# Tail queries of the last layer's attention: four accumulating matmuls per half of the keys, or one matmul per expert whose two halves are added afterwards

## The chip, the cores and the metric

The kernel runs on one core of a Trainium2 chip. The time is the device time of one execution in microseconds (us); the median of three runs of the kernel before is 1179.79 us (1178.86 to 1179.97). Engines are named as in the profile: PE is TensorE (PEld its weight loads), DVE is VectorE, ACT is ScalarE, POOL is GpSimd, SP is SyncE, which here only issues DMAs.

## The reference, cut to what matters

The program computes three layers one after the other: an attention over 32 memory slots, a token and channel mixer, and a mixture of four attention experts. The change lies in the third layer alone:

```python
for e in range(E):                                  # E = 4 experts, B = 8 batches, S = 576, Hd = 64
    q = x @ wq[e]; k = x @ wk[e]; v = x @ wv[e]
    scores = scale * (q @ k.transpose(0, 2, 1))     # 576 x 576 per batch and expert
    scores = np.where(causal, -1e9, scores)         # key j > query i is masked
    a = softmax(scores)
    ye = a @ v @ wo[e]
    out += gate(e) * ye                             # the two best experts of each token
```

Everything is float32. A value is held as a high and a low part (the float32r value that TensorE reads, and the remainder), and a product is built from products of the parts.

## The kernel before, in words

The last layer goes through 32 heads n = 4b + e (batch b, expert e), one per turn t of the loop at the end; a turn scores head t, and transposes and weighs head t-1. Between these steps, `some()` puts in pieces of work that do not belong to the head: the projections to q, k and v, the channel mixer of the next batch (`mm1_2`, `mm2_2`) and the output projection (`project`). The order in which each engine gets its instructions is not the order of the text: the program is built with `schedule_with_timeline_sim=True`, so that a scheduler lays out all engines on a timeline of planned durations and writes the order down; on the chip every engine then follows its written order and waits where an operand is late.

The 576 queries of a head are four blocks of 128 rows (`scores`, c = 0 to 3) and a tail of ST = 64. The tails of two experts, n and n+1 with n even, are handled together, expert n in partitions 0 to 63 and expert n+1 in 64 to 127. There are 16 such pairs.

For one head, `kk` holds the high part of the keys in one half of the partitions and the low part in the other. `qa` holds the queries so that `qa` times `kk` gives high times high plus low times low (the main terms), and `qb` so that `qb` times `kk` gives the two cross products. `tail_queries` (L1346) copies the 64 tail columns of `qa` and `qb` of both experts by four DMAs into `qz`, whose other columns were set to zero once at the start.

`tail_scores(n, hf)` is called for each half (hf) of the 576 keys, 288 columns each. It runs four matmuls into one PSUM tile `s` (L1357): two experts, main and cross terms. Because the other 64 columns of each operand are zero, all four add into one tile. `masked` (L1324) then reads the tile on DVE, adds the causal mask (`cmask`, zero for the first half, `tmask` for the second), scales, writes `ssb` and leaves the row's minimum in `nb`; the second half starts from the first half's minimum. After the second half ACT takes the exponential into `atl` (L1362).

`norm(n)` forms the factor `cf` on DVE (L1370 to L1372) from the sums of all blocks and of the tail and from the gates; POOL multiplies the four blocks of `a` by it (L1380), ACT the tail (L1376). Only then can PE transpose head n's blocks in `turn` (L1399, and L1401 for the last 64 tail columns), in the next turn; `tail_turn` (L1419) transposes the rest of the tail a turn later still.

For e = 2 the two calls of `tail_scores` stand between `scores`, `turn` and `weigh`. For e = 0 they stand between the value projections of a new batch, and the gates are computed after them. PSUM has eight banks here: three for `g`, two each for `t` and `s`, one for `y`.

The lines that the prediction speaks of:

```python
PE.matmul(p[:, 0:SH], lhsT=qz[:, i, x, :], rhs=kk[n + i][:, ks],            # L1357
          start=(i + x == 0), stop=(i + x == 2))
DVE.tensor_tensor_reduce(out=out, in0=p, in1=mask, scale=-scale, ...)       # L1324, masked
ACT.activation(atl[:, 0:S], s_[:], AF.Exp, scale=-1.0, bias=nb[:, 1:2], ...)# L1362
POOL.tensor_mul(x_, x_, cf[:, c:c + 1].to_broadcast([128, W]))              # L1380, norm
```

## Time and profile before

| | us |
|---|---|
| median of 3 runs | 1179.79 (1178.86 to 1179.97) |
| the profiled execution | 1177.93 |
| its span, first to last instruction | 1176.2 |
| PE busy in the span | 1155.9 |
| PEld, DVE, ACT, POOL busy | 1052.5, 785.0, 591.2, 407.8 |
| first and last tail matmul of the last layer (start) | 735.7, 1139.3 |

The profiled execution is 1.86 us below the median, and its span 1.7 us below its own time. Busy time of PE is the union of matmuls whose ends are modelled, so a busy PE can still have a lighter or denser stream of matmuls under it; how densely they follow one another is read from the starts of successive weight loads or matmuls. The granted clock of PE is 0.998 of full speed on the mean over the span.

### The profile page before, as it was taken

Reading aid. Unit: us, or ns where it says so; the run is one execution under the profiler, and the core shown is the slowest. Engines: PE = TensorE matmul, PEld = TensorE weight load, DVE = VectorE, ACT = ScalarE, POOL = GpSimd, SP = SyncE. Lnnn points to the kernel's source line nnn. Section 1 sums busy time; section 2 is a strip of 40 time slices with the busy share of each in tenths; the row PEclk is TensorE's granted clock in tenths of the full one; section 3 lists DMA queues with packets and bytes.
Section 4 is the critical chain, followed back from the end, with each engine's and each line's share of the span. In section 5 each row is a group of like instructions: output and inputs, shape, how many; then the busy total and the mean of one; then the engine's idle time right before and its main releaser. Section 6 shows DMA issues by size and latency. Waiting matters only on the chain.

```text
span 1176.2 us, 23497 instructions
## 1 busy us (share of the span) xinstructions
PE 1155.9 (98%) x8658; PEld 1052.5 (89%) x8658; DVE 785.0 (67%) x1942; ACT 591.2 (50%) x1533; POOL 407.8 (35%) x575
## 2 busy tenths in 40 slices
PE   7999999999999999999999999999999999999998
PEld 6788888888899999999998889999999999999986
DVE  6889998485565665746553624876666777687763
ACT  3566675442322231322221214777677767676774
POOL 3866766000101010100100544647272737373331
PEclk9999999999999999999999999999999999999999
DMA  8999974350121220303110453323332333222423
GB/s 255 248 268 288 285 238 167 133 172 36 38 70 36 72 79 30 108 1 108 37 64 35 131 151 106 90 67 97 77 100 73 103 95 110 70 84 72 151 88 108
DMA packets 125843, 133.53 MB, mean 114 GB/s; under 512 B 36000, under 2 KB 95392, under 8 KB 125728
## 3 DMA queue, kind: packets, MB, share of 16 engines
q1 hardware_dynamic: 125728, 132.03, 37.4%
q8 instruction: 68, 1.11, 0.4%
q14 instruction: 47, 0.39, 0.1%
HBM read 89.01 MB, written 31.46 MB: 102 GB/s over the span
## 4 chain that ended last, share of the span: by engine, by line
PE 83%; DVE 8%; DMA 2%; POOL 2%; issue 2%; ACT 2%; SPq 0%; ACTq 0%; DVEq 0%; POOLq 0%
PE g L251 24%; PE o L251 21%; PE h L251 19%; PE y L1444 4%; PE s L1335 3%; PE t L1399 3%; PE s L1357 1%; POOL a L1380 1%; PE g L677 1%; DVE cm L780 1%; DMA cst<-in_moe_w_tok_dram 1%; PE t L251 1%; PE g L680 1%; PE g L678 1%; PE g L671 1%
## 5 line engine op out<-in xcount | busy, mean ns | idle before, releaser
L983 POOL TENSOR_TENSOR tl<-ub,th 128x512 fp32r<-128x512 f32 x12 | 18.5, 1561 | 362.3 <-DVE tl L983 313.1
L251 PE MATMUL o<-hl,w2h 128*128 128x512 f32 x360 | 141.1, 392 | 0.0
L251 PE MATMUL o<-hh,w2l 128*128 128x512 f32 x360 | 140.4, 390 | 0.0
L251 PE MATMUL o<-hh,w2h 128*128 128x512 f32 x360 | 135.0, 392 | 0.0
L1380 POOL TENSOR_TENSOR a<-a,cf 128x128 f32<-128x128 f32 (+3 forms) x128 | 88.1, 721 | 69.0 <-DVE cf L1372 65.2
L935 ACT ACTIVATE hh<-m 128x256 fp32r<-128x256 f32 x120 | 48.9, 417 | 125.1 <-DVE m L1006 66.1
L1324 DVE CUSTOM_DVE_ANT_0 ssb<-s,cmask 128x128 f32<-128x128 f32 (+2 forms) x144 | 68.5, 483 | 25.2 <-PE s L1335 17.2
L1337 ACT ACTIVATE a<-ssb,nb 128x128 f32<-128x128 f32 (+3 forms) x128 | 71.4, 558 | 19.0 <-DVE nb L1324 14.9
L251 PEld LDWEIGHTS o<-hh,w2l 128*128 128x128 f32 x360 | 67.7, 188 | 14.5
L251 PEld LDWEIGHTS o<-hh,w2h 128*128 128x128 f32 x360 | 67.7, 189 | 12.3
L251 PEld LDWEIGHTS o<-hl,w2h 128*128 128x128 f32 x360 | 67.9, 189 | 11.9
L251 PE MATMUL h<-uh,w1l 128*128 128x256 f32 (+2 forms) x232 | 76.7, 332 | 0.0
L251 PE MATMUL h<-uh,w1h 128*128 128x256 f32 (+2 forms) x232 | 76.3, 331 | 0.0
L251 PE MATMUL h<-ul,w1h 128*128 128x256 f32 (+2 forms) x232 | 76.2, 332 | 0.0
L936 DVE SCALAR_TENSOR_TENSOR hl<-m,hh 128x256 fp32r<-128x256 f32 x120 | 58.7, 498 | 17.9 <-ACT hh L935 15.2
L251 PE MATMUL g<-xh,qkh 128*128 128x288 f32 x232 | 65.5, 301 | 0.0
L1236 POOL TENSOR_TENSOR xl<-p,xh 128x288 fp32r<-128x288 f32 x60 | 47.5, 810 | 49.5 <-ACT xh L1235 49.4
L251 PE MATMUL g<-xh,qkl 128*128 128x288 f32 x232 | 64.1, 296 | 0.0
L999 ACT ACTIVATE m<-h 128x256 f32<-128x256 f32 x30 | 11.5, 384 | 101.4 <-PE h L251 101.4
L1001 DVE TENSOR_TENSOR m<-m,h 128x256 f32<-128x256 f32 x30 | 12.6, 421 | 70.8 <-PE h L251 70.2
L258 DVE TENSOR_TENSOR Bl<-t,Bh 128x512 fp32r<-128x512 f32 (+1 forms) x80 | 50.5, 633 | 13.1 <-ACT Bh L255 12.1
L255 ACT ACTIVATE Bh<-t 128x512 fp32r<-128x512 f32 (+1 forms) x80 | 43.9, 552 | 14.8 <-PE t L1399 6.0
(332 smaller groups left out, 3816.5 us busy)
## 6 DMA issues: line engine op xcount, KB each, us to landing
cst<-in_moe_w_ch_dram SPq DMA_DIRECT2D x24, 512.0 KB, 4.0
u_d<-u SPq DMA_DIRECT2D x32, 288.0 KB, 3.1
ub<-u_d SPq DMA_DIRECT2D x9, 1024.0 KB, 5.0
u<-u_d SPq DMA_DIRECT2D x16, 576.0 KB, 4.1
p<-x_d SPq DMA_DIRECT2D x15, 576.0 KB, 4.0
qn<-in_q_dram SPq DMA_DIRECT2D x16, 512.0 KB, 5.5
kv<-in_k_dram SPq DMA_DIRECT2D x16, 512.0 KB, 5.8
kv<-in_v_dram SPq DMA_DIRECT2D x16, 512.0 KB, 5.6
```

The costliest lines, as they stand in the source:

```text
L251: PE.matmul(ps, lhsT=a, rhs=b, start=start and i == 0, stop=stop and i == len(seq) - 1)
L255: ACT.activation(hi, src, AF.Copy)
L258: DVE.tensor_sub(lo, src, f(hi))
L935: ACT.activation(hh, c, AF.Relu)
L936: DVE.scalar_tensor_tensor(hl, c, 0.0, f(hh), op0=OP.max, op1=OP.subtract)
L1236: POOL.tensor_sub(xl[b][:, c, ss], x_, f(xh[b][:, c, ss]))
L1324: DVE.tensor_tensor_reduce(out=out, in0=p, in1=mask, scale=-scale, scalar=least, op0=OP.add, op1=OP.min, accum_out=acc)
L1335: PE.matmul(p[:, 0:W], lhsT=q_[n][:, 128 * c:128 * c + 128], rhs=kk[n][:, 0:W], start=(i == 0), stop=(i == 1))
L1337: ACT.activation(a[:, aoff[c]:aoff[c] + W], s_[:, 0:W], AF.Exp, scale=-1.0, bias=nb[:, 0:1], accum_out=sm[:, c:c + 1])
L1380: POOL.tensor_mul(x_, x_, cf[:, c:c + 1].to_broadcast([128, W]))
L1399: PE.transpose(p[:, 128 * kc:128 * kc + 128], a[:, o + 128 * kc:o + 128 * kc + 128], ident[:])
L1444: PE.matmul(p[:, lo:w], lhsT=v_[:, kc, 0, :], rhs=x, start=(i == 0), stop=(i == len(ops) - 1))
```

## The change

Each expert's tail operand becomes one tile of 128 columns: main terms (from `qa`) in one half of the columns, cross terms (from `qb`) in the other. One matmul per expert gives both, main in the half of the partitions where that expert's tail belongs and cross in the other half. ACT copies the cross half out of PSUM into a new SBUF tile `cross`, in the partitions of the main half; `masked` then takes that tile where it took the mask. Keys 0 to 511 need no mask for the tail queries, so parts 0 and 1 (one expert each, 512 columns) have none; part 2 (keys 512 to 575 of both experts, 64 columns each in one PSUM tile) has POOL add a 64-column mask to the copied terms first. The zero fill of `qz` goes, and `tmask` shrinks to 64 columns. `tail_scores` is called three times instead of two: for e = 2 the third right after the second, for e = 0 after one more value projection.

```diff
-        tmask = wk_.tile([128, SH], F32, name="tmask")
-        POOL.tensor_copy(tmask[0:ST, :], cmask[0:ST, SH:S])
-        POOL.tensor_copy(tmask[ST:128, :], cmask[ST:128, SH + ST:S + ST])
-        qz = wk_.tile([128, 2, 2, 128], F32R, name="qz")
-        POOL.memset(f(qz[:]), 0.0)
+        tmask = wk_.tile([128, ST], F32, name="tmask")
+        POOL.tensor_copy(tmask[0:ST, :], cmask[0:ST, SM:S])
+        POOL.tensor_copy(tmask[ST:128, :], cmask[ST:128, S:S + ST])
+        qz = wk_.tile([128, 2, 128], F32R, name="qz")
...
-                    SP.dma_start(f(qz[:, i, x, ST * i:ST * i + ST]), f(q_[n + i][:, SM:S]))
+                    o = ST * (x ^ i)
+                    SP.dma_start(f(qz[:, i, o:o + ST]), f(q_[n + i][:, SM:S]))
-        def tail_scores(n, hf):
+        def tail_scores(n, part):
-            if hf == 0:
-                tails[n] = (wk_.tile([128, S], F32, name="ssb", bufs=2), wk_.tile([128, 2], F32, name="nb", bufs=4))
-            s_, nb = tails[n]
-            ks = slice(SH * hf, SH * hf + SH)
+            if part == 0:
+                tails[n] = (wk_.tile([128, S], F32, name="ssb", bufs=2), wk_.tile([128, 2], F32, name="nb", bufs=4),
+                            wk_.tile([128, S], F32, name="cross"))
+            s_, nb, x_ = tails[n]
             p = pp.tile([128, 512], F32, name="s", bufs=2)
-            for i in range(2):
-                for x in range(2):
-                    PE.matmul(p[:, 0:SH], lhsT=qz[:, i, x, :], rhs=kk[n + i][:, ks],
-                              start=(i + x == 0), stop=(i + x == 2))
-            masked(s_[:, ks], p[:, 0:SH], tmask[:] if hf else cmask[:, 0:SH], nb[:, hf:hf + 1],
-                   nb[:, 0:1] if hf else 3.0e38)
-            if hf:
+            ks = slice(0, SM) if part < 2 else slice(SM, S)
+            todo = []
+            for i in (part,) if part < 2 else range(2):
+                o = ST * i
+                c = p[:] if part < 2 else p[:, ST * i:ST * i + ST]
+                PE.matmul(c, lhsT=qz[:, i, :], rhs=kk[n + i][:, ks], start=True, stop=True)
+                ACT.activation(x_[o:o + ST, ks], c[ST - o:128 - o, :], AF.Copy)
+                todo.append((slice(o, o + ST), c))
+            if part == 2:
+                POOL.tensor_add(x_[:, ks], x_[:, ks], tmask[:])
+            for h, c in todo:
+                masked(s_[h, ks], c[h, :], x_[h, ks], nb[h, part // 2:part // 2 + 1], nb[h, 0:1] if part == 2 else 3.0e38)
+            if part == 2:
                 ACT.activation(atl[:, 0:S], s_[:], AF.Exp, scale=-1.0, bias=nb[:, 1:2],
                                accum_out=smb[n % 2][:, NQ - 1:NQ])
...
                 tail_scores(t, 1)
+                tail_scores(t, 2)          # e == 2
...
                 tail_scores(t, 1)
                 values(b, 3)
+                tail_scores(t, 2)          # e == 0
                 values(b, 4)
```

## Rows read from the trace of the kernel before

**Rows 1.** The page, part 1: busy us (share of the span) xinstructions of each engine.
```profile
PE 1155.9 (98%) x8658; PEld 1052.5 (89%) x8658; DVE 785.0 (67%) x1942; ACT 591.2 (50%) x1533; POOL 407.8 (35%) x575
```
**Rows 2.** Windows, last layer: length, busy of each engine, clock, DMA share, GB/s.
```profile
900.00:960.00 60.00, 60.00 (x449) 58.45 (x448) 42.69 (x134) 42.62 (x125) 29.85 (x46) 1.00 0.34 100
...
1150.00:1176.20 26.20, 20.35 (x112) 16.86 (x110) 8.66 (x19) 11.09 (x25) 4.14 (x7) 1.00 0.32 111
sum 486.20, PE 476.11 PEld 457.84 DVE 329.15 ACT 331.31 POOL 231.58; mean PE 47.61 PEld 45.78 DVE 32.91 ACT 33.13 POOL 23.16
```
**Rows 3.** PE's waits from 727 us on, longest of seven lines: total us, times, longest.
```profile
PE g L251 <- ACT osb L1497: 1.3, 3, 0.7
```
**Rows 4.** Timeline, weight loads of one pair's eight tail matmuls: start, us, instruction.
```profile
735.57 1.11 PEld L1357 LDWEIGHTS s<-kk,qz 128*128 128x128 f32 x8
736.62 0.19 PEld L251 LDWEIGHTS g<-hh,w2h 128*128 128x128 f32 x1
```
**Rows 5.** Timeline, a 64-column matmul, 512-column ones behind it, and their weight loads.
```profile
1140.40 0.22 PE L1444 MATMUL y<-Bt,vhl 128*128 128x64 f32 x1
1140.42 0.19 PEld L251 LDWEIGHTS g<-woh,yh 128*128 128x128 f32 x1
1140.45 0.48 PE L251 MATMUL g<-woh,yh 128*128 128x512 f32 x1
1140.53 0.19 PEld L251 LDWEIGHTS g<-wol,yh 128*128 128x128 f32 x1
...
1140.77 0.19 PEld L251 LDWEIGHTS g<-woh,yh 128*128 128x128 f32 x1
```
**Rows 6.** Groups by form, ACT and POOL: busy us, mean ns of one | idle before.
```profile
L1497 ACT ACTIVATE osb<-g 128x512 f32<-128x512 f32 x33 | 19.6, 597 | 13.3 <-DMA out_dram<-osb 5.9 <-PE g L251 5.4 <-ACT a L1337 0.5
...
L1281 ACT ACTIVATE vh<-g 64x64 fp32r<-64x64 f32 x8 | 1.6, 206 | 0.0
...
L1463 POOL TENSOR_TENSOR yel<-yt,yeh 128x64 fp32r<-128x64 f32 x16 | 5.3, 328 | 9.7 <-ACT yeh L1462 9.7
```
**Rows 7.** Groups by form, DVE, line of `masked`: the blocks' and the tail's.
```profile
L1324 DVE CUSTOM_DVE_ANT_0 ssb<-s,cmask 128x512 f32<-128x512 f32 x32 | 21.9, 685 | 0.8 <-PE s L1335 0.4
...
L1324 DVE DVE_READ_ACCUMULATOR2_ANT nb<- 128x1 f32 x160 | 13.2, 82 | 0.0
...
L1324 DVE CUSTOM_DVE_ANT_0 ssb<-s,cmask 128x128 f32<-128x128 f32 x32 | 9.3, 290 | 14.5 <-PE s L1335 14.0
L1324 DVE CUSTOM_DVE_ANT_0 ssb<-s,tmask,nb 128x288 f32<-128x288 f32 x16 | 8.2, 513 | 5.1 <-PE s L1357 4.8
L1324 DVE CUSTOM_DVE_ANT_0 ssb<-s,cmask 128x288 f32<-128x288 f32 x16 | 7.3, 454 | 3.9 <-PE s L1357 3.6
```
**Rows 8.** ACT's waits from 727 us on: total us, times, longest.
```profile
ACT kk L1256 <- DVE kk L1257: 6.5, 12, 1.6
```
**Rows 9.** Timeline of PE, second half of pair 8's tail scores.
```profile
838.41 0.56 PE L1357 MATMUL s<-kk,qz 128*128 128x288 f32 x3
...
839.93 0.38 PE L1357 MATMUL s<-kk,qz 128*128 128x288 f32 x1
```
**Rows 10.** Timeline of pair 8 (e = 0): the tail's sum on ACT, the factor on DVE.
```profile
841.60 0.19 ACT L1362 ACTIVATION_READ_ACCUMULATOR atl<-ssb,nb 128x1 f32 x1
...
850.56 0.16 DVE L1372 TENSOR_TENSOR cf<-cf,gate 128x5 f32<-128x5 f32 x1
```
**Rows 11.** Timeline of pair 30 (e = 2): factor, products, first transposes.
```profile
1142.38 0.17 DVE L1372 TENSOR_TENSOR cf<-cf,gate 128x5 f32<-128x5 f32 x1
...
1142.69 2.75 POOL L1380 TENSOR_TENSOR a<-a,cf 128x128 f32<-128x128 f32 x4 [6.84 <-DVE cf L1372]
...
1146.01 0.49 PE L1399 MATMUL t<-ident,a 128*128 128x128 f32 x3
```
**Rows 12.** Timeline, POOL at the layer's start: the pause after its fills.
```profile
703.03 0.81 POOL L1236 TENSOR_TENSOR xl<-p,xh 128x288 fp32r<-128x288 f32 x1 [11.26 <-ACT xh L1235]
```
**Rows 13.** Windows, 5 us from the first tail matmul of pair 2 (e = 2).
```profile
749.50:754.50 5.00, 5.00 (x40) 5.00 (x39) 4.29 (x12) 4.50 (x12) 5.00 (x8) 1.00 0.00 0
```

## The prediction

> **What bounds the kernel now.** I read the page's engine totals first: PE is busy 98% of the span, DVE 67%, ACT 50%, POOL 35% [rows 1]. Busy time alone is no proof, so next came the table of windows over the last layer, where the whole change lies. A window from its middle has PE busy 60.00 of 60 us, DVE and ACT about 42.6 each, POOL 29.9, with the clock at 1.00; only the last 26 us have PE at 20.35 [rows 2]. Then the waits: from 727 us to the end PE waits for another engine in seven groups, the longest of them 1.3 us in all [rows 3]. So in this layer time is what PE's written order takes to stream, matmul behind matmul, and the other engines have some 30% of room. A matmul taken away is time taken away, as long as what feeds PE is not made late.

> **What goes from PE.** Each of the 16 pairs has eight tail matmuls of 288 columns. Their duration (about 0.3 us) overlaps, so the price is the distance of their starts: the eight weight loads begin at 735.57 and the next instruction's at 736.62 [rows 4], 1.05 us a pair.

> **What comes to PE.** Two matmuls of 512 columns and two of 64. Loads of successive 512-column matmuls stand 0.24 us apart (1140.53 to 1140.77) [rows 5]: 0.48 a pair. For 64 columns there is a low and a high end. The only such matmul has its successor start 0.05 us after it (1140.40, 1140.45), but two loads in a row never stand closer than 0.11 there (1140.42, 1140.53) [rows 5], and two small ones in a row pay that. I take 0.08, between, since the second will often be apart from the first (below): 0.16 for two, 0.10 to 0.22. The sum is 0.64 (0.58 to 0.70) a pair, 0.41 saved (0.35 to 0.47), over 16 pairs **6.6 us (5.6 to 7.5)**.

> **What comes to the other engines.** ACT gets two copies of 64x512 and two of 64x64 out of PSUM. The nearest rows are 0.597 us for 512 columns and 0.206 for 64 [rows 6]: 1.61 us a pair, 26 in all. DVE loses 0.454 + 0.513 and two accumulator reads of 0.082; it gets two reductions over 512 columns at 0.685, two over 64, and four reads. The 64-column one is the 128-column row less 64 columns at the slope of the rows (0.395 us for 384 columns), 0.22 [rows 7]. That is 1.13 against 2.14, 1.0 more a pair, 16 in all. POOL gets one add of 128x64, 0.33 like the subtraction of that size [rows 6], 5 in all. The layer's sums go from 329 to 345 on DVE, 331 to 357 on ACT and 232 to 237 on POOL, of 486 us [rows 2]. None becomes the bound; I cost them at nothing because PE's stream covers them. With the cover gone they would cost at most what they are, 26 us by ACT.

> **Other edits.** The zero fill and the larger mask copies go from POOL at the layer's start; POOL then sits idle 11.26 us anyway [rows 12], so nothing either way. The four DMAs of a pair carry the same 64 columns each over the same queue. The new `cross` tile has one buffer, but pairs are over 10 us apart, so no pair waits for the last one's.

> **The added waits.** In part 2 ACT's first copy stands between the two small matmuls, and both work on one PSUM tile. Does the program keep the second matmul off while ACT reads other columns of it? ACT's copy of one expert's keys (L1256) waits 6.5 us for DVE's read of the other partitions of the same tile, from which it needs no value [rows 8], so yes: PE will wait there, with all later matmuls in its order behind it. The scheduler can put other work into that place, as it did in pair 8, where the second half's first three matmuls began at 838.41 and the fourth at 839.93 [rows 9]. If nothing is put there, the stop is a matmul of 0.22 [rows 5] and a copy of 0.206 [rows 6], 0.43 us a pair at least. I take 0.15 as given back per pair, near the covered end because rows 3 and 9 show covered waits, **2.4 us** in all (0 to 6.9 or more).
> [...]

> The second added wait is in the chain from the tail scores to the factor. Before, a reduction of 0.51 and its read of 0.08 followed the last matmul, 0.9 with that matmul's 0.3. After, it is matmul 0.22, copy 0.21, matmul 0.22, copy 0.21, add 0.33 and two reductions with reads, 0.60, together 1.8, and three more hand-overs at about 0.14 (1142.55 to 1142.69, factor to POOL [rows 11]): 1.3 us later. For e = 0 the tail's sum is ready at 841.8 and the factor is formed at 850.56, since the gates come last [rows 10]: 8.8 us hide it. For e = 2 the products end at 1145.44 and the transposes start at 1146.01 [rows 11], 0.57 us; whether PE then has something else decides the first rival.

> **Sum.** -6.6 + 2.4 = -4.2 us. From the profiled execution's 1177.93 that is 1173.7; this lies 1.86 below the median of the runs, so against the median **1175.6**.

> **Rivals.**
> 1. *The readers eat it.* For e = 2 the other engines are locally full: in 5 us from pair 2's first tail matmul DVE is busy 4.29, ACT 4.50, POOL 5.00 [rows 13], and 1.0, 1.6 and 0.33 come on top. If the transposes are late by 1.3 - 0.57 = 0.73 us for the eight pairs with e = 2 and PE has nothing to put there, 5.8 us come back: 1179.0. For it: the small reserve. Against it: PE never idles there now, and the projections between heads are free to move up. [...]
> 2. *The stop inside part 2 stays open (slower).* PE arrives at the second small matmul before ACT has copied, with nothing between. To the bare 0.43 comes what ACT still has in hand: it is busy 42.62 us in 125 instructions [rows 2], 0.34 each, one whole one ahead and on the mean 71% of half another, 0.12. 0.89 a pair, 14.2 in all: 1179.8 - 6.6 + 14.2 = 1187.4. It decides from 0.41 us a pair on, where the saving is used up. For it: the order is written from planned durations, and ACT runs late against PE in some places. Against it: three matmuls between would cover it, and the scheduler knows the wait.
> 3. *The order of the whole layer is laid out anew*, since three calls stand for two, and comes out better or worse by itself. What better could bring is bounded by PE's 10.1 us without work in this layer [rows 2], of which over half lies in the last 26 us behind a chain that the change does not touch; I put at most 1 us on it below, and for worse the two rivals above stand.

> **How the numbers follow.** Forecast 0.60, first rival 0.26, second 0.14; the third is a spread on each. A change of 0.2%, 2.4 us, is about what can be told from none: faster is below 1177.4, slower above 1182.2. The forecast's own range goes from all of 7.5 us with nothing given back, and 1 us of better order, 1171.3, to 1177.4. To reach 8 in 10 it must take in the first rival with its spread, to 1181.5; the second is left out. So faster 0.60, the same 0.26, slower 0.14.

> **What would show it.** Right: 64 tail matmuls in place of 128, their loads 0.24 and 0.05 to 0.11 us apart; PE's waits in the layer within 3 us of now; PE still full to 1130 us, everything after the first pair progressively earlier by about 0.25 us a pair. First rival: PE idle before transposes, released by POOL or DVE's factor, for e = 2 alone. Second: a wait of PE at the tail matmuls, released by ACT's copy to `cross`, some 16 times at over 0.4 us. I am wrong altogether if PE's idle time does not rise and the time still does not fall, for then the stream's distances are not what rows 4 and 5 say.

## The result and the profile after

The changed kernel takes 1187.17 us (median of 6 runs, 1183.64 to 1188.70), the kernel before 1178.82 beside it: ratio 1.0063, 95% interval [1.005, 1.0075], **slower by about 7.4 us**. Forecast was 1175.6, so the sign was wrong and the time lies outside the range. The profiled execution took 1184.08 us, its span is 1182.4 against 1176.2. It is one of the two fastest of the six; both have a mean granted clock of 0.998, the other four 0.994 to 0.997 and 1185.99 to 1188.70 us. So a part of the 7.4 us may be time at the lower clock, which no trace here shows; what follows is about the 6.2 us between the profiled spans.

The page's totals of the changed kernel, engine by engine:
```profile
span 1182.4 us, 23499 instructions
...
PE 1154.0 (98%) x8594; PEld 1045.7 (88%) x8594; DVE 801.8 (68%) x2006; ACT 618.1 (52%) x1597; POOL 411.9 (35%) x590
```
64 matmuls are gone, and DVE and ACT have grown by about what was worked out. The time must therefore lie where PE stands still. The table of windows over the last layer, of the kernel after (busy us and instructions per engine, PE clock last but two):
```profile
...
727.00:780.00 53.00, 49.72 (x367) 47.64 (x366) 41.56 (x134) 39.08 (x113) 28.62 (x45) 1.00 0.31 86
780.00:840.00 60.00, 57.29 (x414) 54.59 (x415) 43.79 (x143) 46.59 (x135) 30.63 (x48) 1.00 0.30 82
840.00:900.00 60.00, 60.00 (x443) 58.25 (x443) 43.47 (x142) 47.44 (x135) 30.59 (x48) 1.00 0.32 87
...
960.00:1020.00 60.00, 58.08 (x435) 56.05 (x434) 44.69 (x151) 45.83 (x136) 31.37 (x50) 1.00 0.31 87
1020.00:1080.00 60.00, 57.71 (x429) 55.30 (x428) 48.60 (x164) 47.28 (x141) 32.78 (x53) 1.00 0.27 76
...
1130.00:1150.00 20.00, 17.61 (x99) 14.55 (x98) 14.15 (x54) 16.07 (x43) 6.50 (x11) 1.00 0.35 104
1150.00:1182.40 32.40, 26.85 (x152) 22.44 (x150) 12.56 (x29) 16.71 (x39) 7.31 (x12) 0.98 0.32 114
sum 492.40, PE 472.97 PEld 449.69 DVE 346.06 ACT 357.52 POOL 235.93; mean PE 47.30 PEld 44.97 DVE 34.61 ACT 35.75 POOL 23.59
```
Three of the same windows in the kernel before:
```profile
727.00:780.00 53.00, 53.00 (x408) 52.34 (x407) 41.68 (x138) 38.93 (x117) 28.03 (x43) 1.00 0.33 90
780.00:840.00 60.00, 59.81 (x445) 58.08 (x443) 41.09 (x131) 41.98 (x124) 30.68 (x47) 1.00 0.30 82
...
1130.00:1150.00 20.00, 19.70 (x122) 17.20 (x122) 12.84 (x43) 16.62 (x44) 6.25 (x9) 1.00 0.38 124
```
Against [rows 2]: PE's busy time in the layer fell by 3.1 us (476.11 to 472.97) and its time without work rose from 10.1 us (486.2 - 476.11) to 19.4 (492.4 - 472.97), 9.3 more. 9.3 - 3.1 = 6.2, the whole difference of the spans. In this execution the clock is at 1.00 as long as PE has matmuls (the 0.98 of the last window comes from its last 4.4 us, at 0.85, where PE has none), so it has no part in this. The added idle time stands in five windows (727, 780, 960, 1020 and 1130), not in all: from 840 to 900 PE is as full as before. DVE's sum is 346.06 (345 worked out), ACT's 357.52 (357), POOL's 235.93 (237).

PE's waits from 727 us on, kernel after: total us, times, longest. In [rows 3], the kernel before, the longest was 1.3:
```profile
PE g L251 <- DVE qb L1259: 3.5, 4, 1.0
PE g L251 <- DVE p L1233: 2.7, 2, 1.4
PE y L1450 <- ACT Bh L255: 2.3, 3, 1.0
PE g L251 <- ACT osb L1503: 1.6, 3, 0.9
PE t L1405 <- DVE Bl L258: 1.0, 3, 0.4
PE s L1360 <- DVE nb L1323: 1.0, 2, 0.8
...
```
No line has PE waiting for ACT's copy to `cross`. PE waits for the ordinary readers: DVE's and ACT's emptying of projections, transposes and scores. How a tail comes to that shows in the timeline behind one, 779 to 783 us of the kernel after:
```profile
778.70 0.59 ACT L1361 ACTIVATE cross<-s 64x512 f32<-64x512 f32 x1
...
779.32 0.60 ACT L255 ACTIVATE Bh<-t 128x512 fp32r<-128x512 f32 x1
779.33 0.68 DVE L1323 CUSTOM_DVE_ANT_0 ssb<-s,cross 64x512 f32<-64x512 f32 x1 [0.34 <-ACT cross L1361]
779.95 0.69 DVE L258 TENSOR_TENSOR Bl<-t,Bh 128x512 fp32r<-128x512 f32 x1
...
780.79 0.52 PE L1405 MATMUL t<-ident,a 128*128 128x128 f32 x3 [0.42 <-DVE Bl L258]
781.05 0.59 ACT L1361 ACTIVATE cross<-s 64x512 f32<-64x512 f32 x1
781.66 0.60 ACT L255 ACTIVATE Bh<-t 128x512 fp32r<-128x512 f32 x1
...
782.31 0.79 PE L1450 MATMUL y<-Bh,vhl 128*128 128x320 f32 x4 [1.01 <-ACT Bh L255]
```
ACT is asked for `Bh`, which PE needs for the next product, and has the copy to `cross` in hand first (781.05, 0.59 us, of PE's stop of 1.01). Likewise an earlier copy (778.70, 0.59) stands ahead of the `Bh` at 779.32; DVE's `Bl` follows that `Bh` within 0.03 us (779.92 to 779.95), and PE, which needs the tile that `Bl` reads, stops 0.42. DVE's half-height reduction at 779.33 holds nothing up here. The new work of the readers is not waited for by name; it makes the old work late. Another kind stands at 1143.81, in the last pair:
```profile
1143.81 0.30 PE L1360 MATMUL s<-kk,qz 128*128 128x64 f32 x1 [0.78 <-DVE nb L1323]
```
Part 2 is a third tile a pair in the ring of two `s` tiles, so its first matmul waits until DVE has read an earlier one. The prediction had not counted that. Other stops lie away from any tail, as this one at 746 us, over 7 us from the nearest tail matmul, where DVE's sum itself waits for a DMA (DVE row first, then PE's):
```profile
747.27 1.18 DVE L1233 TENSOR_TENSOR p<-p,g 128x288 f32<-128x288 f32 x3 [1.52 <-DMA p<-x_d]
...
747.78 0.40 PE L251 MATMUL g<-hh,w2h 128*128 128x288 f32 x1 [1.36 <-DVE p L1233]
```
So there are two candidates: the readers' work, and the order, which was written anew for the whole layer.

### The profile page after: what moved, and what is told of

The parts are those of the page before. It is cut to its first block, busy times and chain, and to the rows that moved or that the text cites. A ratio compares the mean times of both kernels' runs of the same rounds, so it can differ in the third digit from the quotient of the medians.

```text
span 1182.4 us, 23499 instructions
## 1 busy us (share of the span) xinstructions
PE 1154.0 (98%) x8594; PEld 1045.7 (88%) x8594; DVE 801.8 (68%) x2006; ACT 618.1 (52%) x1597; POOL 411.9 (35%) x590
## 4 chain that ended last, share of the span: by engine, by line
PE 84%; DVE 7%; DMA 3%; ACT 3%; issue 1%; SPq 1%; POOL 0%; DVEq 0%; ACTq 0%
PE g L251 23%; PE o L251 21%; PE h L251 19%; PE y L1450 4%; PE s L1334 3%; PE t L1405 2%; PE g L677 1%; PE g L671 1%; PE g L680 1%; PE g L678 1%; PE g L438 1%; DVE ssb L1323 1%; PE t L251 1%; DMA cst<-in_moe_w_tok_dram 1%; PE t L488 1%
## 5 line engine op out<-in xcount | busy, mean ns | idle before, releaser
L1386 POOL TENSOR_TENSOR a<-a,cf 128x384 f32<-128x384 f32 (+3 forms) x128 | 88.4, 724 | 41.0 <-DVE cf L1378 39.5
L1323 DVE CUSTOM_DVE_ANT_0 ssb<-s,cmask 128x128 f32<-128x128 f32 (+3 forms) x128 | 61.4, 485 | 21.2 <-PE s L1334 12.8
L258 DVE TENSOR_TENSOR Bl<-t,Bh 128x512 fp32r<-128x512 f32 (+1 forms) x80 | 50.2, 634 | 14.5 <-ACT Bh L255 13.5
L1457 POOL TENSOR_TENSOR yl<-yt,yh 128x256 fp32r<-128x256 f32 x30 | 22.3, 742 | 97.5 <-ACT yh L1456 97.5
```

The costliest lines, as they stand in the source:

```text
L258: DVE.tensor_sub(lo, src, f(hi))
L1457: (DVE if n == NE - 1 else POOL).tensor_sub(yl[:, ym], yt[:, ym], f(yh[:, ym]))
```

## The experiments

Differences are (ratio - 1) x 1178.8 us, each against the runs of the kernel before on the same chip; an interval is some 1.5 us to either side. What is read from a trace holds for the one profiled execution.

**How an order is held.** Experiments "in an order" add, at the program's end, edges without semaphores from each instruction of the last layer outside the tail scores to the one that precedes it on its engine in the other kernel:
```diff
+        for eng, text in ORDER.items():
+            step = np.frombuffer(zlib.decompress(base64.b85decode(text)), "<i2")
+            row = [kept[eng][k + int(d)] for k, d in enumerate(step)]
+            for a, b in zip(row, row[1:]):
+                tc.add_manual_dep(b, a.name, mybir.DependencyInfo(mybir.DependencyClass.NoSync,
+                                  mybir.DependencyReason.DATA), reason="order")
```
The tail scores themselves are placed by the scheduler. In e11 and e12 the traces have the tail's matmuls at the same places among PE's other matmuls as in the kernel before, in e9 and e13 to e15 nearly so. No run holds the order without any other edit, so what the holding costs by itself is not measured; e9, held, is still 6.0 us faster.

### Order alone, copies alone, rival 2

**e1_before_new_order**: the old work, everything else of the layer in the new kernel's order.

> The kernel before, with all work of the last layer outside the tail scores put into the order that the changed kernel has on every engine (the tail scores themselves are placed by the scheduler). Theory A, order: the new order is what costs; PE has its old 128 tail matmuls back, so the time is that of the changed kernel (1187) or up to 7 us above it, 1185 to 1194. Theory B, readers: the copies of the cross terms and the longer reductions cost, and they are not here: 1177 to 1181. Between them, 1181 to 1185, would say both have a part.

1185.16 us, ratio 1.0051 [1.0037, 1.0065]: +6.0, the lower edge of theory A. With not one instruction of the change, this order costs that much, and PE's longest waits are of the new kernel's kinds:
```profile
PE g L264 <- DVE p L1249: 2.5, 3, 1.1
PE g L264 <- DVE qb L1275: 2.2, 3, 1.0
PE y L1466 <- ACT Bh L268: 1.6, 4, 0.6
```
PE's time without work in the layer is 13.6 us here (491.7 - 478.07) against 10.1.

**e2_after_old_order**: the new work, the rest in the old order (on PE, ACT and DVE).

> The changed kernel with all work of the last layer outside the tail scores in the order of the kernel before, on PE, ACT and DVE (the tail scores are placed by the scheduler). Theory A, order: the saved matmuls show, 1170 to 1176. Theory B, readers: their load stands beside the same work, so PE stops as in the changed kernel: 1183 to 1190.

1244.72 us, 1.056 [1.0546, 1.0574]: +66, far outside both theories. PE's longest waits by the tail's ring and the copies:
```profile
PE s L1347 <- DVE nb L1336: 19.6, 17, 2.6
PE s L1373 <- ACT cross L1374: 4.9, 5, 1.6
```
The old order has room for two `s` tiles a pair, not for three: 17 times a block's score matmul waits for its tile, each time behind one of the tail's reductions. (e15 below, with the copies and the halves but two tiles, has 4.9 us in five such waits.) What the rest of the 66 us is made of was not taken apart. Here, in an order not made for it, rival 2's wait for `cross` does appear, 4.9 us in five.

**e3_no_copies**: the changed kernel without ACT's copies and POOL's add, the cross terms left out, the order free.
```diff
-                ACT.activation(x_[o:o + ST, ks], c[ST - o:128 - o, :], AF.Copy)
-            if part == 2:
-                POOL.tensor_add(x_[:, ks], x_[:, ks], tmask[:])
```

> The changed kernel without ACT's copies of the cross terms and without POOL's add: the reductions take the mask tiles in their place, so the cross terms are left out of the tail scores. The scheduler lays out a new order. Theory B, readers, with ACT as the place: most of the 13 us of added PE stops go, 1170 to 1177. Theory A, order: a new draw of the order, with PE's gain kept, anywhere from 1172 to 1187.

1181.60 us, 1.0023 [1.0013, 1.0033]: +2.7. Without the copies and the add it is 4.7 us better than the changed kernel, but still not faster than before; that the 4.7 are their price is not shown, since the order is another one too. (The profiled execution lost 1.7 us to a dip of the clock, last section.)

**e4_both_first**: both 64-column matmuls ahead of both copies.
```diff
-                ACT.activation(x_[o:o + ST, ks], c[ST - o:128 - o, :], AF.Copy)
                 todo.append((slice(o, o + ST), c))
+            for h, c in todo:
+                ACT.activation(x_[h, ks], c[ST - h.start:128 - h.start, :], AF.Copy)
```

> The changed kernel with both 64-column matmuls of part 2 ahead of both copies, so that PE has no wait for ACT between them. My second rival (the stop inside part 2) expects that its 16 stops go, 1174 to 1178. Theory B expects nothing from it, 1184 to 1190. Theory A, a new draw of the order: anywhere from 1174 to 1190.

1187.81 us, 1.0081 [1.0066, 1.0096]: +9.5. (The profiled execution, 1187.76 us at a mean clock of 0.995, lost 1.7 us to a dip in the layer; three others at 0.998 took 1187.05 to 1187.86, so the dip does not explain the time.) Nothing is won by taking away the stop inside part 2: rival 2 named the time almost to the microsecond (1187.4), but the trace of the changed kernel has no such stop, and here, without a place for it, the time does not fall.

### The new order with parts of the work

**e5_no_copies_new_order** is e3 in the changed kernel's order; **e6_old_plus_copies_new_order** is e1 with four copies a pair added:
```diff
+            for o in (0, ST):
+                ACT.activation(s_[o:o + ST, ks], p[ST - o:128 - o, 0:SH], AF.Copy)
             masked(s_[:, ks], p[:, 0:SH], ...
```

> The changed kernel without ACT's copies and POOL's add (the cross terms are left out of the tail scores), with all other work of the last layer in the changed kernel's own order. The old matmuls in this order took 1185.2 (the first experiment), the changed kernel 1187.2. Theory B1, the copies eat the saved matmul time: without them it shows, 1177 to 1180. Theory B2, what eats it is not the copies but the third tile per pair in the two s banks or the four half-height reductions: 1184 to 1188.

> The kernel before in the changed kernel's order, as in the first experiment (1185.2), and in addition four ACT copies of 64x288 per pair out of the s tile into ssb, ahead of the reductions, which overwrite them: the copies' time on ACT (1.6 us a pair) and the wait of the reductions for them, without the change's matmuls. Theory B1, copies: 1191 to 1196. Theory B2: 1184 to 1188.

e5: 1184.77, 1.0048 [1.0037, 1.0059], +5.7. e6: 1192.32, 1.0115 [1.0101, 1.0128], +13.6. In this order the changed work without its copies in place of the old (e1 to e5) is worth 0.3 us, and copies beside the old matmuls (e1 to e6) cost 7.6; e6's profiled execution lost 3.4 us in two dips of the clock. So e5 falls into B2's range and e6 into B1's, and neither theory holds alone. Against the changed kernel, whose order this is, e5 gains 1.7 us (7.4 to 5.7) by leaving out copies and add, about what the intervals can tell. In e5 PE is busy 6.4 us less than in e1 (471.64 against 478.07) and idle 6.6 us more (20.2 against 13.6): the change's own matmuls do save about the 6.6 us of PE's busy time that the prediction worked out, and what is saved turns into waiting, again mostly for `p` and `qb`.

**e7_neutral_move**: the kernel before with one call put elsewhere; **e8_small_part_first**: the changed kernel with part 2 ahead of parts 0 and 1.
```diff
                 values(b, 2)
-                tail_scores(t, 1)
                 values(b, 3)
+                tail_scores(t, 1)
```

> The kernel before with one call moved: for e = 0 the second half of the tail scores stands after the fourth value projection instead of before it. No work is added or removed. Theory A, order: the order of the kernel before is a good draw and most others are worse, 1180 to 1187. Without theory A: 1177 to 1181.

> The changed kernel with part 2 (64 keys, two copies, POOL's add) ahead of parts 0 and 1, so that the end of the chain to the exponential is one copy and one reduction, and POOL's add is off it. If the length of this chain is what costs: 1174 to 1181. If it is order and the readers' load: a new draw around the changed kernel, 1181 to 1192.

e7: 1180.17, 1.0011 [1.0001, 1.0021], +1.3. e8: 1192.96, 1.0119 [1.0101, 1.0136], +14.0. So not every rearrangement costs 6 us; and with part 2 early, in the order that the scheduler then makes, nothing is won.

### One term at a time, in the old order

Here the kernel before keeps its own order, and one term of the prediction's sum is put in by itself. **e9_half_matmuls_old_order** leaves out the cross-term matmuls, 64 of 128; **e10_half_matmuls_free** is the same with a free order; **e11_copies_old_order** has e6's copies; **e12_half_height_old_order** splits each tail reduction in two.
```diff
-                for x in range(2):
-                    PE.matmul(p[:, 0:SH], lhsT=qz[:, i, x, :], ...
+                PE.matmul(p[:, 0:SH], lhsT=qz[:, i, 0, :], ...              # e9, e10
...
+            for h in (slice(0, ST), slice(ST, 128)):                         # e12
+                masked(s_[h, ks], p[h, 0:SH], ...
```

> The kernel before, in its own order on all engines, with the four cross-term matmuls of each pair left out (so the cross terms are missing from the tail scores): 64 of 128 tail matmuls, 8.4 us of PE's stream at 131 ns each, and no other edit. Theory P, PE's stream bounds this layer in this order: 1170 to 1172. Theory S, the stops are set by other engines and PE only meets them earlier: 1175 to 1179.

> The same as e9 (cross-term matmuls left out, nothing else), but the scheduler lays out the order anew. Theory A, a new order is worse by itself: some us above e9. Theory P without A: like e9, 1170 to 1173.

> The kernel before, all matmuls, in its own order, and in addition four ACT copies of 64x288 per pair from the s tile into ssb, ahead of the reductions, which overwrite them: 1.6 us of ACT a pair and the reductions' wait for it. Theory B, readers: 5 to 10 us, 1184 to 1189. If ACT's room covers them: 1178 to 1181.

> The kernel before, all matmuls, in its own order, with each reduction of a pair made as two of 64 partitions: four in place of two, 1.06 us more of DVE a pair, no copies. Theory B, readers: 2 to 6 us, 1181 to 1185. If DVE's room covers them: 1178 to 1180.

| run | median us | ratio, 95% | us |
|---|---|---|---|
| e9 fewer matmuls, old order | 1173.74 | 0.9949 [0.9936, 0.9961] | -6.0 |
| e10 the same, free order | 1178.73 | 0.9993 [0.9982, 1.0005] | -0.8 |
| e11 copies, old order | 1183.81 | 1.0043 [1.0029, 1.0057] | +5.1 |
| e12 half-height, old order | 1185.52 | 1.0050 [1.0037, 1.0063] | +5.9 |

Most of the saving is there (e9): 6.0 of the 8.4 us, between the two theories, while PE's time without work rises from 10.1 to 12.2. In a free order nearly all of it goes (e10). In the profiled execution most of that stands in one place, a new stop of 2.07 us for a DMA of queries, and a granted clock of half behind it (timeline of PE, then windows):
```profile
1106.73 0.33 PE L1335 MATMUL s<-kk,qa 128*128 128x128 f32 x1 [2.07 <-DMA qa<-qb]
```
```profile
1107.00:1108.00 1.00, 1.00 (x9) 0.95 (x9) 0.79 (x3) 0.45 (x3) 0.00 (x0) 0.94 1.05 282
1108.00:1109.00 1.00, 1.00 (x4) 0.81 (x3) 0.94 (x5) 0.79 (x3) 0.00 (x0) 0.50 1.03 341
...
1110.00:1111.00 1.00, 1.00 (x6) 1.00 (x5) 0.02 (x1) 0.60 (x1) 0.00 (x0) 0.50 0.45 110
1111.00:1112.00 1.00, 1.00 (x9) 1.00 (x8) 0.00 (x0) 0.00 (x0) 0.00 (x0) 0.85 0.85 314
```
0.06 + 3 x 0.50 + 0.15 = 1.7 us of lost speed; with the stop 3.8 of the 5.2 us between e9 and e10. Three of e10's eleven executions, at a mean clock of 0.998 to 0.999 against 0.996 here, took 1176.2 to 1176.6 us, so not every execution loses as much.

Each reader's work costs some 5 us on its own (e11, e12) though the engines are 52% and 68% busy. e11 keeps 26 us of copies hidden but for 5.1, e12 adds 14.1 us to DVE (799.1 against 785.0) and pays 5.9. PE's time without work rises from 10.1 to 13.5 in e11 and to 15.4 in e12. The longest lines of its waits, e11 and then e12, are score matmuls that wait for an `s` tile, and the emptying of output tiles:
```profile
PE s L1350 <- DVE nb L1339: 2.4, 4, 0.8
PE g L264 <- ACT osb L1521: 1.8, 3, 0.8
```
```profile
PE g L264 <- ACT osb L1520: 3.6, 3, 2.5
PE s L1350 <- DVE nb L1339: 1.7, 2, 1.3
```
In the kernel before no score matmul of a block waits for `nb` (the one such wait, 0.3 us, stands at a tail matmul). All four of e11's and both of e12's end behind a reduction of the *tail*, as here in e11: tail matmuls, copies, reduction, and only then the next block's scores:
```profile
1034.58 0.75 PE L1372 MATMUL s<-kk,qz 128*128 128x288 f32 x4
...
1036.68 0.81 ACT L1375 ACTIVATE ssb<-s 64x288 f32<-64x288 f32 x2
...
1037.52 0.52 DVE L1339 CUSTOM_DVE_ANT_0 ssb<-s,tmask,nb 128x288 f32<-128x288 f32 x1 [0.23 <-ACT ssb L1375]
...
1038.10 0.44 PE L1350 MATMUL s<-kk,qa 128*128 128x384 f32 x1 [0.81 <-DVE nb L1339]
```
The added work holds the tail's `s` tile longer, and with two such tiles in all the next block must wait for it. In e12 the longest wait lies elsewhere: 2.5 us at 1178 us, some 30 us behind the last tail, where an output tile waits for its DMA (0.4 us there before). Whether the halves bring that about is not shown; without these 2.1 us e12's price would be nearer to 4, which is what they cost in e14 against e9 (4.3).

### Do the terms add up?

-6.0 + 5.1 + 5.9 = +5.0, short of +7.4. The last four put the terms together: **e13_cut_and_copies_old_order** (e9 with e11's copies), **e14_cut_and_half_height_old_order** (e9 with e12's halves), **e15_all_three_old_order**, and **e16_all_three_free_order**, e15's work with the order free. Their diffs are those above.

> The kernel before in its own order, with the cross-term matmuls left out (64 of 128) and four ACT copies of 64x288 a pair added ahead of the reductions. Alone the first gave -6.0 us and the second +5.1. Theory A (the effects add): -0.9 us against before, about 1178.5. Theory B (PE, 8.4 us less to stream, reaches the same late readers earlier, so that the copies eat the saving and more): over +1 us, 1180 or more. Theory C (the copies only cost where PE's stream is full, and the cut makes room): -3 us or lower.

> The kernel before in its own order, with the cross-term matmuls left out and each tail reduction split in two of 64 partitions. Alone -6.0 and +5.9 us. Theory A (add): -0.1 us, about 1179. Theory B (the saving is eaten and more): over +2. Theory C (room made by the cut): -3 or lower.

> The kernel before in its own order with all three edits: cross-term matmuls left out, four copies, reductions in halves. Theory A (add): -6.0 + 5.1 + 5.9 = +5.0, about 1184.2. Theory B: more than that, 1187 or above, so that the whole loss of the changed kernel is there without a new order. Theory C: the readers share their stops, 1179 to 1182.

> The same three edits, with the order laid out by the scheduler. If the new layout costs about 5 us on top, as it did for the cut alone, this stands 4 to 6 us above the same work in the old order. If the scheduler, knowing the copies and the halves, places them better than the old order can, it stands below it. If it is at the changed kernel's 1187, the three-part split (a third tile in the ring of two) has no price of its own in a free order.

| run | median us | ratio, 95% | us | sum of the terms |
|---|---|---|---|---|
| e13 | 1180.76 | 1.0022 [1.0012, 1.0032] | +2.6 | -0.9 |
| e14 | 1177.17 | 0.9986 [0.9977, 0.9994] | -1.7 | -0.1 |
| e15 | 1189.91 | 1.0094 [1.0081, 1.0107] | +11.1 | +5.0 |
| e16 | 1183.32 | 1.0035 [1.0023, 1.0047] | +4.1 | |

They do not add. The cut with the copies is worse than the sum (3.5 us), with the halves about the sum (1.6 better, near what the intervals can tell), and all three are 6.1 worse. (A sum of three such differences is uncertain by some 2.6 us.) A part of that excess shows in e15's windows around 816 us:
```profile
814.00:815.00 1.00, 0.13 (x1) 0.00 (x0) 0.56 (x2) 0.95 (x4) 1.00 (x3) 1.00 0.00 0
815.00:816.00 1.00, 0.86 (x7) 0.89 (x8) 1.00 (x5) 0.61 (x3) 1.00 (x2) 0.91 0.00 0
816.00:817.00 1.00, 1.00 (x6) 1.00 (x5) 0.60 (x3) 1.00 (x5) 1.00 (x3) 0.50 0.07 16
...
818.00:819.00 1.00, 1.00 (x5) 1.00 (x5) 0.41 (x1) 0.23 (x1) 1.00 (x3) 0.50 0.00 0
819.00:820.00 1.00, 1.00 (x8) 1.00 (x7) 0.94 (x4) 0.75 (x3) 0.75 (x1) 0.88 0.00 0
```
PE had two stops in a row (0.82 and 1.01 us, below), and behind them the granted clock fell from 1.00 to 0.50 of full speed for over 3 us: 0.09 + 3 x 0.50 + 0.12 = 1.7 us of lost speed, as in e10. The stops themselves come from the first rival's chain at an e = 2, by a way that the rival did not name. DVE waits 1.01 us for the tail's sum before the factor, and `Bl` stands behind it in DVE's order; ACT waits 1.26 us for the factor, and `Ah` stands behind its product. PE's next transposes need the tiles that `Bl` and `Ah` read:
```profile
812.10 0.17 DVE L1393 TENSOR_SCALAR cf<-sm 128x5 f32<-128x5 f32 x1 [1.01 <-ACT atl L1378]
...
812.53 0.56 DVE L271 TENSOR_TENSOR Bl<-t,Bh 128x384 fp32r<-128x384 f32 x1
...
813.23 0.63 PE L1422 MATMUL t<-ident,a 128*128 128x128 f32 x4 [0.82 <-DVE cf L1395]
...
813.25 0.78 ACT L1399 ACTIVATE atl<-atl,cf 128x576 f32<-128x576 f32 x1 [1.26 <-DVE cf L1395]
...
813.93 0.47 ACT L268 ACTIVATE Ah<-t 128x384 fp32r<-128x384 f32 x1
...
815.14 0.52 PE L1422 MATMUL t<-ident,a 128*128 128x128 f32 x3 [1.01 <-DVE Al L271]
```
The profile puts the first of PE's stops down to the factor, which ended last; but POOL's products with it begin only at 813.24, so these transposes do not need it, and `Bl` ends at 813.09, 0.14 us ahead of them. The remaining 4.4 us of e15's excess are not pinned to one place; the waits for the tail's `s` tile are the longest line again (`PE s L1350 <- DVE nb L1339: 4.9, 5, 1.3`).

e16 bears on the order. For the same three edits the free order is 7 us *better* than the old one, while for the cut alone it was 5 us worse (e10 against e9). The layout is not a fixed tax: the scheduler's own order for the work at hand was worse than the old one in one case and better in the other, and the same work swings by 5 to 7 us between two orders. e16 has 8.4 us of matmuls less than before (64 x 1.05/8, [rows 4]), the copies and the halves, in two tiles a pair, and stands at +4.1. The changed kernel (+7.4) differs from it by the three-part split, POOL's add, the wider pieces (by the prediction's own sum they save 6.6 us in place of 8.4) and, again, its layout: some 3 us with an uncertainty of 2, of which the ring's wait (`PE s L1360 <- DVE nb L1323`, 1.0 us of PE, above) is the part that a row shows.

## Why the prediction was wrong, point by point

- **What bounds the layer.** Right as far as it went: PE's written order sets the time. "The other engines have some 30% of room" was read as room at every place. It is a mean: where a tail falls, [rows 13] had shown the engines full.
- **What goes from PE and comes to PE.** Right in kind: with 64 matmuls left out, 8.4 us by the distances of [rows 4], and the order held, e9 falls by 6.0 [4.6, 7.5]. The change's own 6.6, with its two 512-column and two 64-column matmuls a pair, fits what PE's busy time loses from e1 to e5 in one order (6.4); as time it shows there with 0.3 us only.
- **What comes to the other engines: this is the step that failed.** "None becomes the bound; I cost them at nothing because PE's stream covers them." Their durations were as worked out: a copy 0.592 and 0.218 us on the mean, a half-height reduction 0.69 over 512 columns; only the 64-column one is 0.28 in place of 0.22. But in the old order copies alone cost 5.1 us and half-height reductions alone 5.9, some 20 to 40% of the work given to each engine (with the doubt on 2.1 us of e12 above). Neither engine is the bound; but the added work keeps the tail's `s` tile from the next block's scores and stands ahead of reads that PE waits for next, so PE's stream did not cover it.
- **The third tile.** Not in the sum. e2 priced what it does in an order without a place for it (19.6 us of PE's waits at the ring, where e15 with two tiles has 4.9); in the changed kernel a wait of 1.0 us is left of it.
- **The stop inside part 2** (2.4 us) and **rival 2**: no PE wait for `cross` in the changed kernel, and e4 gains nothing. Each time other work covered it. The number 1187.4 was hit by chance, and a single run without the trace would have seemed to confirm it.
- **Rival 1, the readers eat it**: the right family, too small and at the wrong place. It had one chain, the factor for e = 2, priced at 5.8 us; e15 shows that chain at one place, and there through `Bl` and `Ah`, which stand behind the factor on DVE and ACT, not through the products; the changed kernel waits mainly for `Bh`, `Bl`, `qb`, `p`. In the traces the tail matmuls fell from 128 to 64, while ACT and DVE, which empty their tiles, have 26.2 and 16.9 us more in the layer.
- **Rival 3, the order anew, "at most 1 us".** Wrong by a factor of five to seven: equal work in two orders differs by 6.0 (before, e1), 5.2 (e9, e10) and 7.0 us (e15, e16), of the last two 1.7 each by the clock in the profiled executions; e7's rearrangement, a smaller one, costs 1.3. Its bound was taken from PE's idle time in the old layout, which limits what a better order could gain, and for a worse one nothing was counted.
- **What would have told.** The prediction named "PE's waits within 3 us of now" as its test; the time without work rose by 9.3, so the trace answers as the text had asked, against the forecast. Idle time did rise, so the distances of [rows 4] and [rows 5], the last thing that the text put in doubt, are not refuted.

Open: how the 7.4 us split between readers and order in the changed kernel itself, since the two are not independent, how much of it the lower clock of four of its six executions makes, and which of its differences from e16 holds the last 3 us.

## What to carry to other kernels

When one engine streams 98% of the time in a fixed order, work moved from it to engines that are "only" half or two thirds busy need not be free: here 26 us and 14 us of work that was to be covered cost 5 to 6 us each, about as much as the whole saving. In this kernel the price was a fifth to two fifths of the added length; for another it is a first guess until an experiment in the fixed order says otherwise. Look at the local windows and not at the mean, and ask which tile the added work keeps from the busy engine: here the next block's scores waited for the tail's. And before a difference of half a per cent is put down to an edit, hold the order and make the edit alone: two layouts of the same work lay 5 to 7 us apart here, either way.

## What the runs showed of the hardware

Half the partitions did not halve a reader's time here: a reduction over 64 partitions and 288 columns took 0.514 us in e12, over 128 partitions 0.513 in the kernel before [rows 7], and ACT's copy of 64x512 took 0.592 us in the changed kernel against 0.597 for 128x512 [rows 6].
